# Outer products of batch 0 moved to GpSimd, two late stores moved to its queue, and a new hand-written order, in a fused sketch attention and swish layer

## The chip, the cores and the metric

The kernel runs on 1 core of one Trainium2 chip. The metric is the device time of one execution in microseconds. The profiled execution is described by its own span and its own time.

## The reference

```
q, k, v: (4, 4, 1088, 32) f32      S1, S2: (8, 32)
phi(x)[i, j] = (S1 x)[i] * (S2 x)[j]          # 64 features for each row of 32
kv  = sum_s phi(k)[s] (x) v[s]                # 64 x 32 for each batch and head
z   = sum_s phi(k)[s]
attn = phi(q) . kv / (phi(q) . z + 1e-6)
x   = attn, heads side by side                # (4352, 128)
h   = x @ w_in                                # w_in (128, 2048)
out = (h * sigmoid(beta * h)) @ w_out         # w_out (2048, 128), beta (2048)
```

## The kernel before

The work has two halves that run interleaved on one core: the attention of four batches, and the layer with w_in and w_out over nine chunks of tokens (eight of 512, a last one of 256), each chunk as soon as the attention has given its tokens.

All five engines are scheduled by hand. The string `ORDER` near the end of the kernel (line 919 on) lists short tokens; each token issues the instructions of one step, and every engine executes its own instructions in the order in which the tokens stand. A token late in the string can still run early, when its engine has nothing before it, and an engine waits at the first instruction whose inputs or buffers aren't ready.

The layer's tokens, each counted up by itself (W3.5 is the sixth of chunk 3):

- `W`: TensorE (PE) multiplies a chunk by columns of w_in (two matmuls of 128x512, or four of 128x256) into `wave`, L396. The PSUM pool `psm` behind it has two buffers, and `qps`, `nps` and others take theirs from it too, so a W waits for the silu, or the attention's read, two allocations back.
- `G`: ScalarE (ACT) takes the silu of one wave into an f16 tile `g`, L425 (L417 for the last). Six such tiles exist.
- `V`: PE multiplies `g` by w_out into the accumulator `moeout`, L470 (L459 and L448 for the last chunk).
- `O`: VectorE (DVE) turns a finished chunk into `o_sb`, L506, and `store` issues its DMAs, L380: one for each of four groups of 32 partitions, in packets of 128 B. A chunk that crosses batches has eight. The last chunk, tokens `O8`, is copied instead (`o_u`, L494) and stored by two DMAs, one on ACT's queue and one on SP's (L495).

The attention's tokens, with the batch in the first digit:

- `lk`, `lq`, `lv` load k, q and v on SP's queue (L109, L125). A tiny POOL memset ahead of each load (L108, L120, L122) holds it back until POOL has come that far; `lo`, `li` do so for the weights (L140, L136).
- `tk`, `tq`: DVE turns k or q (L521, L527). `kp`: PE's `kps`; `kt`: DVE turns it into `kab` (L569); `oKbn`: the outer product phi(k), a quarter each (L581, two or three rows of 128x256); `kv`: PE's `kvz` (L593). `gm`, `gc`, `wz`, `wc`: a Gram matrix (L607), its copy (L619), a product with it (L625) and the copy of that into `qw` (L634).
- `kd`, `no`, `ni`: DVE turns `kvz` (L638), SP writes it to DRAM (L643) and reads it back four times as `nd` (L652).
- `qp`: PE's `qps` from `qT` and `qw` (L660); `qa`: DVE turns it, two halves (L672); `dt`, `ds`, `sa`: the denominator and the scaling by it (L680, L690 and L693, L698); `oqbn`: the outer product phi(q), in parts of 128x512 or 128x768 (L705; batch 0 has two parts, the others four); `tbn`: DVE turns each part into `qt` (L715); `nm`: PE's `nps` from `qt` and `nd` (L732); `x`: two casts into `xT`, the layer's input (L747; L745 and L756 in batch 3).
- `wi`, `wo` scale parts of the weights; `cl` is eight POOL memsets (L208, L210, L212) that clear the padding of `kTs`, `pac` and `qw`; `sq` copies S1 and S2 into `qw` (L271).

A letter at the end of a token is the engine: v is DVE, c is ACT, g is GpSimd (POOL). The first 512 tokens of batch 0 take a short cut that isn't touched.

Of the kernel before, what the change touches and what calls it, by code (L numbers as in the profile page):

```python
# [20 lines left out]
def kernel(  # L21
# [12 lines left out]
    nc = tc.nc  # L34
# [52 lines left out]
    def sb(shape, dtype, name):  # L87
        return const.tile(shape, dtype, tag=name, name=name)
# [97 lines left out]
    mk = sb([P, H, R], F32, "mk")  # L186
# [168 lines left out]
    LASTC = len(tok_chk) - 1  # L355
# [17 lines left out]
    def store(o_sb, t0, u0, u1, queues):  # L373
        c = t0 + 32 * u0
        while c < t0 + 32 * u1:
            b, r = divmod(c, S)
            n = min(t0 + 32 * u1 - c, S - r) // 32
            u = (c - t0) // 32
            for g4 in range(4):
                queues[g4 % len(queues)].dma_start(  # L380
                    out=bass.AP(
                        tensor=out.tensor,
                        offset=out.offset + (b * S + r // 32) * DM + 32 * g4,
                        ap=[[T * DM, 32], [DM, n], [1, 32]],
                    ),
                    in_=o_sb[32 * g4 : 32 * g4 + 32, u : u + n, :],
                )
            c += n * 32
# [90 lines left out]
    def turn_out():  # L479
        ci = moe["o"]  # L480
        t0, tw = tok_chk[ci]
        nt = tw // 32
        if ci == LASTC:

            acc = moe["acc"].pop(0)
            b, r = divmod(t0, S)
            ns = P // nt
            for n, ((a, e), (cp, eng)) in enumerate(
                zip(LASTU, ((VC, nc.scalar), (VC, nc.sync)))
            ):  # L490
                u, p0 = divmod(a, P)
                p1 = p0 + e - a
                o_u = sbG1.tile([P, DM], F32, tag=f"o_u{n}", name=f"o_u{n}")
                cp(out=o_u[p0:p1], in_=acc[u][p0:p1, :P])  # L494
                eng.dma_start(  # L495
                    out=bass.AP(
                        tensor=out.tensor,
                        offset=out.offset + (b * S + T * (ns * u + p0 // nt) + r // 32) * DM,
                        ap=[[T * DM, (p1 - p0) // nt], [DM, nt], [1, DM]],
                    ),  # L500
                    in_=o_u[p0:p1],
                )
            moe["o"] += 1
            return
        o_sb = sbA.tile([P, TCH // 32, 32], F32, tag="o_sb", name="o_sb")
        nc.vector.transpose(  # L506
            out=o_sb[:, :nt, :].rearrange("p t d -> p (t d)"), in_=moe["acc"].pop(0)[:, :tw]
        )
        store(o_sb, t0, 0, nt, [nc.sync])
        moe["o"] += 1  # L510


# [335 lines left out]
    def x_A(i):  # L848
# [4 lines left out]
    V, C, G = nc.vector, nc.scalar, nc.gpsimd  # L853
# [11 lines left out]
        "s0": spread_sq,  # L865
        "xp": lambda: put_last(VC),
        "W": w1, "G": silu, "V": w2, "O": turn_out,
    }
    for e, eng, cp in (("v", V, VC), ("c", C, CC), ("g", G, GC)):
# [35 lines left out]
    for b in range(B):  # L905
# [14 lines left out]
                DO[f"kv{b}{j0}{j1}"] = lambda b=b, j0=j0, j1=j1: kv(b, j0, j1)  # L920

    ORDER = """
        cl h lqB tk00 h h h h h h h S0 Sbv Sc h h tk01 h rb rv bb by3c by2c mk tqA j2 j1 y2v y1c by0v ok04v
        j0 y0c by1c gm0 Spg Ssg s0 q00 q10 ok08g ok02v q01 ok00v ok01v kv002 gt ok03v gc0v zm li1 lm lk
        ok05g q11 tqB zc kv024 sq0 wi0v sq3 lk1 ok07g ok06g kv046 kv068 kv089 wi1v sq1 wi3g lo0 wi5g dA0 iA0
        kqc nq kd0 nc dA1 nA0 wi4g xA0 wi2g no0 lq1 lo1 iA1 nA1 sq2 W G wz0 wc0v xA1 wi7g tk1 W G wi6g ni0
        qp0 wo0g qa00 qa01 W W G kp1 lv1 W dt0v ds0 wo1g wo3g kt1 sa0g oq01v wo2c tq1 oq00g oK12g V V t01
        gm1 G G W gc1c wz1 lk2 lq2 V wc1c t00 qp1 V G qa10 qa11 wo4c oK10v oK11v wo5c dt1v oK13g W G V V
        wo7g W G nm0 x00c x01c ds1 sa1v kv109 kd1 no1 W oq13g ni1 oq11g lv2 W wo6c V V lk3 G W tk2 O t13 G
        kp2 kt2 G W G V W G V oq10g t10 W G gm2 W G oq12v oK21g V t11 t12 oK20g tq2 oK23v W G lq3 V nm1 gc2c  # L930
        wz2 V V x10c wc2v qp2 x11c W qa20 V oK22g V W G W G G tk3 O qa21 kv209 kd2 W lv3 no2 V W kp3 G dt2v
        ds2 G ni2 W kt3 V sa2g oq23v G W G V oq22v W G V W gm3 W V G G W V oq20g G W oK32v t22 tq3 V t20 V O
        W oK30g gc3c wz3 G G W V G W G V V W oq21g t21 t23 nm2 oK31g V V G x20c W V x21v wc3v qp3 qa30 G W G
        V V oK33g qa31 dt3g O W G W G kv309 W G W ds3 V V W sa3g V oq31g kd3 no3 G G ni3 t31 W G oq33g t33 V
        W V oq30g W G G V W G V W G V t30 W oq32v t32 nm30 O x30v W G G W V V W V G W G G V W V V G W V W V
        G O G W G nm31 W W G V V G W V V G x31v W W G G V V xp W V W G V W V V G G W G W V V W G G V W G V W
        G V W G V W O V V G V O V O
    """
    for name in ORDER.split():
        DO[name]()  # L940
# [29 lines left out]
```

## Time and profile before

| | |
|---|---|
| runs | 102.74 us median of 3 (102.02 to 103.11) |
| profiled execution | 102.41 us, span 100.6 us |
| busy, share of the span | PE 93%, ACT 76%, DVE 60%, POOL 39% |
| granted TensorE clock | 1.00 throughout |
| first W of the layer | starts at 15.5 us |
| last matmul ends | 96.7 us |
| last packet of a store | 99.1 us |
| HBM | 9.32 MB read, 2.36 MB written |

Times in the profile are microseconds from the start of the span. PE is shown busy from a matmul's start to its modelled end, so that a matmul that follows closely hides small waits; the start-to-start distance of instructions tells more than the busy share. For a DMA, the queue's entry (SPq, ACTq) is the issue; its packets move later.

### The profile page before, as it was taken

To read this page: it belongs to the slowest core of one execution; us is meant where nothing else is said; L and a number is where in the kernel's file an instruction comes from. 1 tells how busy PE (TensorE), PEld (TensorE's weight loads), DVE (VectorE), ACT (ScalarE), POOL (GpSimd) and SP (SyncE) were. 2 spreads that over 40 slices of the span, in tenths; PEclk is the share of its full clock that TensorE was granted. 3 is DMA by queue.
4 is the path that set the end of the run, shared out by engine and by line. 5 is a ranking of instruction groups with operands and counts; after the bars stand their busy time and mean duration, and the time that the engine had idled before them with its cause. 6 is when DMAs were issued, how large, how long until landed. Compare 5 with 4: busy or idle time off the path is not lost.

```text
span 100.6 us, 3192 instructions
## 1 busy us (share of the span) xinstructions
PE 93.1 (93%) x1303; PEld 44.7 (44%) x1303; DVE 60.6 (60%) x122; ACT 76.6 (76%) x100; POOL 39.4 (39%) x76
## 2 busy tenths in 40 slices
PE   6997997895999999999999999999999999999950
PEld 2336744452573444364443434644344444445740
DVE  3479599999999895599999038458230260020220
ACT  0507835788489995599999765999979979999930
POOL 6247769689309991005996003591000000000000
PEclk9999999999999999999999999999999999999999
DMA  2999995893930249985822330511015051014053
GB/s 57 312 214 289 267 349 116 296 266 92 301 148 16 58 132 227 194 228 94 217 42 47 50 55 7 89 30 50 9 18 85 0 84 20 7 22 70 13 87 69
DMA packets 24870, 11.89 MB, mean 118 GB/s; under 512 B 18436, under 2 KB 23316, under 8 KB 24856
## 3 DMA queue, kind: packets, MB, share of 16 engines
q1 hardware_dynamic: 24656, 11.61, 47.3%
q8 instruction: 10, 0.16, 0.7%
q10 hardware_dynamic: 200, 0.08, 0.4%
q14 instruction: 4, 0.03, 0.1%
HBM read 9.32 MB, written 2.36 MB: 116 GB/s over the span
## 4 chain that ended last, share of the span: by engine, by line
PE 52%; DVE 23%; DMA 10%; SPq 5%; issue 3%; ACT 2%; POOL 1%; DVEq 0%
PE wave L396 18%; PE moeout L470 17%; PE h L222 5%; DMA k<-in_k_dram 5%; PE nps L732 4%; SPq L125 4%; DVE qT L527 3%; DMA v<-in_v_dram 3%; DVE qab L672 3%; DVE qt L715 3%; DMA ndd<-kvd 2%; DVE qo L705 2%; SPq L652 2%; PE kvz L593 1%; DVE rc L690 1%
## 5 line engine op out<-in xcount | busy, mean ns | idle before, releaser
L425 ACT ACTIVATE g<-wave 128x1024 f16<-128x1024 f32 x67 | 63.9, 1030 | 10.4 <-PE wave L396 10.1
L396 PE MATMUL wave<-xT,winp 128*128 128x512 f16 (+1 forms) x152 | 39.6, 356 | 0.7 <-DVE xT L849 0.2
L470 PE MATMUL moeout<-g,woutp 128*128 128x512 f16 (+1 forms) x136 | 35.3, 366 | 0.1
L396 PEld LDWEIGHTS <-winp 128*128 128x128 f16 x152 | 13.7, 97 | 18.2 <-issue 8.5
L470 PEld LDWEIGHTS <-woutp 128*128 128x128 f16 x136 | 12.9, 97 | 14.7 <-issue 1.3
L506 DVE STREAM_TRANSPOSE o_sb<-moeout 128x512 f32<-128x512 f32 x8 | 5.6, 706 | 18.2 <-PE moeout L470 18.1
L581 POOL TENSOR_TENSOR kp<-kab 128x512 f32<-128x512 f32 (+2 forms) x12 | 13.2, 1107 | 2.2 <-DVE kab L547 2.2
L705 POOL TENSOR_TENSOR qo<-qab 128x512 f32<-128x512 f32 (+1 forms) x9 | 12.0, 1351 | 4.3 <-DVE qab L698 4.1
L715 DVE STREAM_TRANSPOSE qt<-qo 128x512 f32<-128x512 f32 (+1 forms) x14 | 10.5, 762 | 2.7 <-POOL qo L705 2.6
L732 PE MATMUL nps<-qt,nd 32*32 32x288 f32 (+1 forms) x256 | 6.8, 384 | 0.0
L672 DVE STREAM_TRANSPOSE qab<-qps 128x576 f32<-128x576 f32 (+1 forms) x8 | 5.2, 683 | 2.6 <-PE qps L660 2.6
L705 DVE TENSOR_TENSOR qo<-qab 128x512 f32<-128x512 f32 (+1 forms) x5 | 6.0, 1209 | 0.1
L698 POOL TENSOR_TENSOR qab<-qab,rc 128x288 f32<-128x288 f32 (+1 forms) x3 | 1.8, 609 | 10.1 <-DVE rc L693 10.1
L222 PE MATMUL h<-const-bfloat16-1.0 128*128 128x512 bf16 x11 | 5.0, 625 | 0.8 <-PEq L954 0.8
L527 DVE STREAM_TRANSPOSE qT<-q 128x1088 f32<-128x1088 f32 (+2 forms) x5 | 5.3, 1060 | 0.0
L593 PEld LDWEIGHTS kvz<-kp,v 128*32 128x32 f32 x288 | 4.2, 110 | 2.0 <-issue 0.8
L593 PE MATMUL kvz<-kp,v 128*32 128x64 f32 x288 | 5.1, 221 | 0.0
L310 POOL TENSOR_TENSOR winp<-beta_bc,w_in_sb 128x256 f16<-128x256 f32 x6 | 4.3, 736 | 1.5 <-DMA w_in_sb<-in_moe_w_in_dram 1.5
L732 PEld LDWEIGHTS nps<-qt,nd 32*32 32x32 f32 x256 | 3.4, 103 | 3.2 <-issue 1.3
L660 PE MATMUL qps<-qT,qw 32*32 32x288 f32 (+1 forms) x128 | 3.0, 386 | 1.6 <-ACT woutp L335 1.2
L521 DVE STREAM_TRANSPOSE kTs<-k 128x1088 f32<-128x1088 f32 x3 | 3.9, 1294 | 0.8 <-DMA k<-in_k_dram 0.8
L306 ACT COPY beta_bc<-bb 128x512 f32<-128x512 f32 x3 | 1.7, 588 | 3.4 <-PE bb L301 3.4
(105 smaller groups left out, 75.6 us busy)
## 6 DMA issues: line engine op xcount, KB each, us to landing
v<-in_v_dram SPq DMA_DIRECT2D x12, 144.0 KB, 4.6
k<-in_k_dram SPq DMA_DIRECT2D x3, 544.0 KB, 4.9
q<-in_q_dram SPq DMA_DIRECT2D x3, 544.0 KB, 3.7
out_dram<-o_sb SPq DMA_DIRECT2D x20, 64.0 KB, 2.6
w_in_sb<-in_moe_w_in_dram SPq DMA_DIRECT2D x2, 512.0 KB
w_out_sb<-in_moe_w_out_dram SPq DMA_DIRECT2D x2, 512.0 KB, 4.4
nd<-ndd SPq DMA_DIRECT2D x16, 32.0 KB, 1.8
v<-in_v_dram SPq DMA_DIRECT2D x4, 112.0 KB
```

Source lines behind the costliest of these rows:

```text
L222: nc.tensor.matmul(out=t, lhsT=idle_w, rhs=idle_x, start=True, stop=True)
L396: nc.tensor.matmul(out=wv[:, jj // per, c : c + w], lhsT=winp[:, (j0 + jj) * P : (j0 + jj + 1) * P], rhs=xT[:, t0 + o : t0 + o + w], start ...
L425: nc.scalar.activation(out=g[:, :, :gw], in_=wv[:, :, :gw], func=ACTF.Silu)
L470: nc.tensor.matmul(out=moe["acc"][-1][:, o : o + w], lhsT=woutp[:, j0 + jj, :], rhs=g[jj], start=head and jj == 0, stop=tail and jj == jn - 1,
L506: nc.vector.transpose(out=o_sb[:, :nt, :].rearrange("p t d -> p (t d)"), in_=moe["acc"].pop(0)[:, :tw])
L527: nc.vector.transpose(out=qT2[b % 2][:, t0:t1].rearrange("p t s -> p (t s)"), in_=q_t[b][:, t0:t1].rearrange("p t d -> p (t d)"),)
L581: eng.tensor_tensor(out=cut(KP[b][:, j0:j1], [[F, n], [R, R], [1, R]]), in0=a, in1=cut(KAB[b][:, 1, j0:j1], [[R, n], [0, R], [1, R]]), op=MUL,
L593: nc.tensor.matmul(out=KVZ[b][32 * h : 32 * h + 32, :F], lhsT=v_t[b][:, h, j, :], rhs=KP[b][:, j, h, :], start=(j == 0), stop=(j == NJK - ...
L672: nc.vector.transpose(out=cut(QAB[b], [[32, 2], [32 * H, nq], [1, 32]], 64 * pr), in_=PS["qps"][pr][:, :, : 32 * nq],)
L705: eng.tensor_tensor(out=cut(QO[b][:, j0:j1], [[F, n], [R, R], [1, R]]), in0=cut(a0, [[32, n], [1, R], [0, R]]), in1=cut(a0, [[32, n], [0, ...
L715: nc.vector.transpose(out=QT[b][:, j0:j1].rearrange("p j h c s -> p (j h c s)"), in_=QO[b][:, j0:j1].rearrange("p j h f -> p (j h f)"),)
L732: nc.tensor.matmul(out=t[g // 2][32 * h : 32 * h + 32, g % 2, : 32 * nq], lhsT=ND[b][rows, h, 32 * fc : 32 * fc + 32], rhs=QT[b][rows, :nq ...
```

## The change

Three edits, in one diff:

- The stores of the last chunk but one (`ci == LASTC - 1`, chunk 7) alternate between SP's queue and POOL's, two each. All other stores stay on SP's.
- In the order, both outer products of q of batch 0, `oq00` and `oq01`, stand on POOL, one behind the other; `oq01` was on DVE, ahead of `tq1`, the turning of batch 1's q.
- The rest of the order is new. No step is added or left out; some change their engine and most change their place. `cl` goes from the very start to just before `qp0`; `sq2` goes to the start; `wc0` and `wo1` go from DVE and POOL to ACT, `wo2` and `wo6` from ACT to POOL and DVE, `wo7` from POOL to ACT; the outer products of batch 3's q go to DVE altogether, while those of batch 2 and several of k change sides; `x21` goes from DVE to ACT; `lq2` is separated from `lk2`; chunk 0's stores come ahead of the loads of batch 2's v on SP's queue; `xp` stands just before W8.0.

```diff
@@ -506,7 +506,7 @@
-        store(o_sb, t0, 0, nt, [nc.sync])
+        store(o_sb, t0, 0, nt, [nc.sync, nc.gpsimd] if ci == LASTC - 1 else [nc.sync])
@@ -920,21 +920,21 @@
     ORDER = """
-cl h lqB tk00 h h h h h h h S0 Sbv Sc h h tk01 h rb rv bb by3c by2c mk tqA j2 j1 y2v y1c by0v ok04v
+h lqB tk00 h h h h h h h S0 Sbv Sc h h tk01 h rb rv bb sq2 by3c by2c mk tqA j2 j1 y2v y1c by0v ok04v
         j0 y0c by1c gm0 Spg Ssg s0 q00 q10 ok08g ok02v q01 ok00v ok01v kv002 gt ok03v gc0v zm li1 lm lk
-ok05g q11 tqB zc kv024 sq0 wi0v sq3 lk1 ok07g ok06g kv046 kv068 kv089 wi1v sq1 wi3g lo0 wi5g dA0 iA0
-kqc nq kd0 nc dA1 nA0 wi4g xA0 wi2g no0 lq1 lo1 iA1 nA1 sq2 W G wz0 wc0v xA1 wi7g tk1 W G wi6g ni0
-qp0 wo0g qa00 qa01 W W G kp1 lv1 W dt0v ds0 wo1g wo3g kt1 sa0g oq01v wo2c tq1 oq00g oK12g V V t01
-gm1 G G W gc1c wz1 lk2 lq2 V wc1c t00 qp1 V G qa10 qa11 wo4c oK10v oK11v wo5c dt1v oK13g W G V V
-wo7g W G nm0 x00c x01c ds1 sa1v kv109 kd1 no1 W oq13g ni1 oq11g lv2 W wo6c V V lk3 G W tk2 O t13 G
-kp2 kt2 G W G V W G V oq10g t10 W G gm2 W G oq12v oK21g V t11 t12 oK20g tq2 oK23v W G lq3 V nm1 gc2c
-wz2 V V x10c wc2v qp2 x11c W qa20 V oK22g V W G W G G tk3 O qa21 kv209 kd2 W lv3 no2 V W kp3 G dt2v
-ds2 G ni2 W kt3 V sa2g oq23v G W G V oq22v W G V W gm3 W V G G W V oq20g G W oK32v t22 tq3 V t20 V O
-W oK30g gc3c wz3 G G W V G W G V V W oq21g t21 t23 nm2 oK31g V V G x20c W V x21v wc3v qp3 qa30 G W G
-V V oK33g qa31 dt3g O W G W G kv309 W G W ds3 V V W sa3g V oq31g kd3 no3 G G ni3 t31 W G oq33g t33 V
-W V oq30g W G G V W G V W G V t30 W oq32v t32 nm30 O x30v W G G W V V W V G W G G V W V V G W V W V
-G O G W G nm31 W W G V V G W V V G x31v W W G G V V xp W V W G V W V V G G W G W V V W G G V W G V W
-G V W G V W O V V G V O V O
+ok05g wi1v q11 tqB zc kv024 sq0 wi0v sq3 lk1 ok07g ok06g kv046 kv068 kv089 sq1 wi3g lo0 wi5g dA0
+wi4g iA0 kqc nq kd0 nc wi2g dA1 nA0 xA0 no0 lq1 iA1 nA1 wi6g xA1 lo1 wi7g W G W wz0 ni0 wc0c cl qp0
+tk1 wo0g qa00 wo3g G qa01 dt0v lv1 W W kp1 wo1c G wo2g W G G V V ds0 kt1 sa0g oq00g oq01g gm1 lk2
+gc1c W G oK13g wz1 wo5c V wo4c tq1 wc1v qp1 t00 W G V t01 V oK11g V qa10 W G qa11 nm0 x00c x01c
+oK10v oK12v kv109 W dt1v lq2 ds1 sa1g wo6v oq12g W wo7c V V kd1 no1 G G ni1 tk2 O W lv2 oq11g G kp2
+W G V lk3 t11 W G kt2 V oq13g oq10g t13 W gm2 W oK20g V G W V G G gc2c t12 t10 tq2 nm1 wz2 x10c V V
+wc2v x11c W oK21g qp2 V G V qa20 W O W qa21 dt2v G oK23g oK22g kv209 kd2 no2 ni2 G W V ds2 W G G V
+sa2v oq23g tk3 oq22v W V V t22 W G V oq20v G W kp3 kt3 oK31g oq21g W G G V W V G W G lq3 lv3 V O W
+t20 G gm3 W G V W t23 V V W t21 G nm2 G oK33g gc3c wz3 W wc3v x20c x21c oK32v G V V W G V tq3 qp3
+qa30 qa31 W oK30g G V V O dt3g ds3 W G W kv309 G W W kd3 V V no3 G G W V sa3v oq33v W V G oq32v ni3
+W V V oq31v G G W V W G G V W oq30v t30 t33 t32 t31 nm30 W G G O W G V V W V W V G G x30v W V W G G
+V W G V W G V O W nm31 x31v G W G W V G V W V W G V G W V V W G W V V G W V G G W V W V V G O G W G
+V xp W G V W G V W G V W O V G V V V O
```

## The prediction

> **What bounds the kernel now.** I read the page's first part, then the idle time of each engine by stretches, then the timeline of the stretch where TensorE (PE) still stands idle, and last the tail. One silu (ACT, L425, the token G) handles what one W (L396) made; one V (L470) uses it. The page:
>
> ```profile
> PE 93.1 (93%) x1303; PEld 44.7 (44%) x1303; DVE 60.6 (60%) x122; ACT 76.6 (76%) x100; POOL 39.4 (39%) x76
> ```
>
> PE is the fullest engine. The table by stretches (length, then busy time and count of PE, PEld, DVE, ACT, POOL; granted clock, DMA share, GB/s):
>
> ```profile
> 44.00:56.20 12.20, 12.12 (x90) 4.91 (x89) 11.26 (x17) 11.77 (x14) 7.97 (x6) 1.00 0.48 114
> 73.00:95.30 22.30, 22.30 (x141) 10.60 (x140) 4.47 (x6) 20.63 (x23) 0.00 (x0) 1.00 0.22 35
> ```
>
> The clock is 1.00 throughout. From 44 on ACT is nearly as full as PE (11.77 of 12.20): a W and a V take 0.43 us each on PE, 0.86 together, a silu 0.93 to 0.95 (8 in 7.60). So there the silus set the pace, and PE catches up where products of the attention hold it. An earlier start of the stretch moves both engines alike, and what is gained before it should reach the end. The one large hole of PE lies before it, in the timeline of PE:
>
> ```profile
> 22.50 0.61 PE L470 MATMUL moeout<-g,woutp 128*128 128x256 f16 x4
> 24.32 0.78 PE L660 MATMUL qps<-qT,qw 32*32 32x288 f32 x32 [1.21 <-ACT woutp L335]
> ```
>
> V0.2 ends near 23.0 and qps of batch 1 (qp1) starts at 24.32. The profile names an ACT copy that ended then, but qps also reads qT of batch 1; the timelines of DVE and POOL, and the chain that ended last, show that this was late:
>
> ```profile
> 20.21 0.85 DVE L569 STREAM_TRANSPOSE kab<-kps 128x288 f32<-128x288 f32 x2
> 20.98 1.97 DVE L705 TENSOR_TENSOR qo<-qab 128x512 f32<-128x512 f32 x1
> 22.87 1.30 DVE L527 STREAM_TRANSPOSE qT<-q 128x1088 f32<-128x1088 f32 x1
> 24.10 1.52 DVE L715 STREAM_TRANSPOSE qt<-qo 128x512 f32<-128x512 f32 x2
> ```
> ```profile
> 20.90 1.51 POOL L705 TENSOR_TENSOR qo<-qab 128x768 f32<-128x768 f32 x1
> 22.36 1.52 POOL L581 TENSOR_TENSOR kp<-kab 128x512 f32<-128x512 f32 x1
> ```
> ```profile
> 21.05 1.90 DVE qo L705
> 22.95 1.22 DVE qT L527
> 24.17 1.45 DVE qt L715 x2
> ```
>
> The outer product oq01 runs on DVE ahead of the turning of q (tq1) and takes 1.97 us beside POOL's oq00; the same 128x512 product took DVE 0.65 us at 68.82, when POOL was idle. The turning ends at 24.17, qps starts 0.15 later.
>
> **The change, part by part.**
>
> *oq01 to POOL, tq1 right after kt1.* DVE loses 1.97 ahead of tq1. tq1 now runs 21.05 to 22.3 (1.25 us, rows of L527); q of batch 1 is there (its packets landed by 19.0). wz1 must end first: W0.5 and wz1 by about 22.4, wc1 by 22.6, V0.2 by 22.85, so qp1 starts near 22.85 in place of 24.32: 1.47 earlier. On POOL oq01 comes behind oq00 (20.90 to 22.41) and ends at 23.45 (1.04 to 1.07, the undisturbed 128x512 rows). Behind it on POOL come oK13 (1.51, to 25.0) and oK11 (1.05, to 26.05), while DVE has oK10 and oK12, to 26.9. kv1 needs all four; before they were ready at 28.1 and kv1 started at 28.41. PE now goes qp1 (0.70) 23.55, W0.6 24.0, V0.3 24.43, V0.4, held to 24.65 by the ACT copies wo5, wo4 (0.65 each behind G0.5), V0.5 and W0.7 by 25.95, nm0 (1.11) from 25.95 to 27.06, kv1 from there. Its inputs: t00 22.6 to 23.5, t01 to 24.25, the two qab to 25.65; v of batch 1 landed by 24.8, nd by 22.4. Gain at nm0: 27.30 - 25.95 = 1.35.
>
> *The clears of POOL (cl) moved from 2.63 to about 17.0.* Eight memsets, 0.49 us in the trace (2.63 to 3.12). At the start POOL waited 1.88 us for st anyway: worth nothing. Now they stand behind wi6, wi7 (two at 0.70, 15.62 to 17.02) and end near 17.5; qps of batch 0 and the turning of k (tk1) wait for them. qps starts at 17.5 in place of 17.21, but its readers (qab) wait on DVE for tk1, which ends at 18.35 as before: 0 to 0.15 lost. The cover is those 0.4 us of tk1. The copy wc0 goes from DVE (0.13) to ACT (0.17, between two silus): W0.2 moves from 18.12 to 18.3, but W0.3 waits for the first qab (18.8) either way. sq2 (0.19) now precedes sk and spm on POOL; spm ends by 6.3, and its user starts at 9.28: nothing.
>
> *The new order after that.* Same instructions, moved. I went by hand through the places where an input may come late, with the rows' durations.
> - nm1: POOL does sa1, oq12, oq11, oq13, oq10 in a row from 28.35 (0.65, 1.07, memsets 0.4, 1.07, 1.51, 1.07: 34.2); the last turn ends at 35.3; PE arrives at 35.35. Start 35.4 for 37.04: 1.6 gained, with no margin.
> - SP's queue: k and q of batch 2 no longer go together, q follows oK11 at 26.1, ahead of no1 at 28.9: free. Chunk 0's stores (four at 0.55) now stand ahead of v and k of batches 2 and 3: v then lands near 39.4 (issue 35 to 38; before 38.5), kv2 starts at 41.3: covered by 1.9. tk3, which waited 0.84 us for k before, stands later on DVE.
> - kv2 ends at 42.5 for 43.89 (1.4). Then silus set the pace: G2.3 starts at 43.0 for 44.53 (1.5).
> - nm2 waits for oq21, on POOL behind oK31, which waits for kt3 on DVE: 48.85, 49.9, 51.0, its turn 53.1; PE arrives at 53.7. Covered by 0.6, which DVE products slowed by POOL (1.2 for 0.9, twice) would use up.
> - Batch 3: all four outer products on DVE, POOL idle by then: 0.95 + 3 x 0.65 from 62.85, turns to 68.6; PE reaches nm30 at 69.0. If POOL's absence didn't help (1.27 each, the mean of L705 DVE 128x512) nm30 would wait 1.5 us.
> This gives 1.4 to 2.0 at these places. It grants every handover at the trace's best, so I count 1.4 from the first stage and 0.3 from the order.
>
> *Two stores of chunk 7 on POOL.* The tail:
>
> ```profile
> 95.39 1.95 SPq L380 DMA_DIRECT2D out_dram<-o_sb  x4
> 97.43 0.61 SPq L495 DMA_DIRECT2D out_dram<-o_u  x1
> ```
> ```profile
> 96.69 0.52 DVE L494 COPY o_u<-moeout 128x128 f32<-128x128 f32 x2 [1.33 <-PE moeout L448]
> ```
>
> The last store is issued 0.22 after its copy ended (97.21), as SP is busy until 97.34. With two stores fewer it goes out at 97.27: 0.16 gained, perhaps 0.3, since its packets then stand behind 1024 others of 128 B and not 2048. The price of a store issued by POOL is in no row. Lower end: SP's median, 0.46 us. Upper end: 2.0, the longest instruction of either vector engine on a 128x512 tile (1.97). I take 1.07, POOL's own time for 512 elements a partition, as a store has 512 packets. SP's last packet left 1.24 us after its last issue ended (98.58 after 97.34), so POOL's would leave at 95.4 + 2 x 1.07 + 1.24 = 98.8, just ahead of the last packet of all (99.14): nothing lost, and the 0.15 stays. At 2.0 it is 100.6: 1.5 lost.
>
> A rule of the Trainium skill speaks against this part: "DMA: Bandwidth & Descriptors", section "Issuing engines are not separate DMA queues", says that stores of any engine end on the same 16 DMA engines, and that spreading them only saves issue time; its Specifications give about 1 us to the first byte for POOL's path and 0.6 for SP's. By that the part is worth at most the 0.16 and may cost an estimated 0.4 us at the start of POOL's packets, which the 0.3 us of slack above nearly hides.
>
> **Sum.** 1.4 + 0.3 + 0.15 = 1.85 off the profiled execution's 102.41 (span 100.6 and 1.8 around it, unchanged): 100.56. It lies 0.33 under the median of the runs, 102.74, so 100.9 in such a median. With the bounds: from 2.3 gained to, with POOL's stores at 2.0 each, 0.2 gained.
>
> **Rivals.**
> 1. *The gain is taken back* by new waits at nm1, nm2 and nm30 (no margin, 0.6, 0.4): two of them late by 0.5 to 0.8 leave 1.85 - 1.2 = 0.65: 102.1. For: POOL's and DVE's products ran at 1.27 on the mean and not at 1.07 and 0.65. Against: in this order fewer of them overlap. 0.21.
> 2. *POOL's stores set the end* (slower). Their place is the last 5 us, with nothing behind them to hide in. From 1.25 us each they end after today's last packet; from 2.1 us they have eaten the gain; at 3.0 the end is 96.64 + 6.0 = 102.64 for 99.14, 3.5 later, less 1.7: 104.5. For: no row bounds them. Against: POOL's elementwise work on as many elements takes half of that. 0.12.
> 3. *The stall doesn't go*: qp1 really waited for the ACT copies, which the profile names. They then end at 24.6, qp1 starts no earlier, and only about 0.45 remains: 102.3. Against: qps reads nothing that they write. 0.05.
>
> **How the numbers follow.** The forecast, 100.9 (own range 100.0 to 101.6), has 0.62. A measurement tells about 1% from no change, 1.03 us. Faster by more: 0.62 and a little of rival 1, 0.64. Within 1%: most of rivals 1 and 3, 0.23. Slower: rival 2 and a little beside, 0.13. The range, 99.9 to 102.9, takes in rivals 1 and 3 and POOL's stores up to 2.2 us each; the slow end of rival 2 is left out.
>
> **What would show it.** Right: PE's hole before the second qps under 0.3 us, that qps near 22.9, the first nps near 26, the second near 35.4, nm2 near 53.8; the last o_u store issued within 0.1 of its copy, POOL's two stores under 1.2 us each. Wrong: a hole of over 0.5 us ahead of a later nps or kvz, ACT with as many gaps after 44 as now, or a last packet that is POOL's.

## The result, and the profile after

The changed kernel takes 101.58 us in the median (100.70 to 104.44, 22 runs), the kernel before 102.19 us (101.16 to 103.91, 22 runs) beside it. The ratio is 0.994, with a 95% interval of 0.9919 to 0.9962: faster by 0.6%, where the forecast was 1.8%. The profiled execution took 101.3 us (span 99.5), 1.1 us under that of the kernel before, and the forecast for it was 1.85. So even the two profiles differ by more than the medians do. In some executions the full TensorE clock comes several us later than in others; the ratios leave these out, and below places are counted from the first W of the layer, which takes most of that out.

The page of the changed kernel, busy time by engine, and the table by stretches (columns as before):

```profile
PE 92.0 (92%) x1303; PEld 44.7 (45%) x1303; DVE 58.2 (58%) x123; ACT 77.2 (78%) x101; POOL 37.6 (38%) x76
```
```profile
44.00:56.20 12.20, 12.18 (x149) 5.29 (x147) 7.56 (x12) 11.10 (x14) 6.55 (x8) 1.00 0.40 107
73.00:95.30 22.30, 22.30 (x159) 11.24 (x157) 3.79 (x5) 21.00 (x24) 0.98 (x2) 1.00 0.23 37
```

DVE lost 2.4 us and the picture is otherwise the same: PE is the fullest engine, and in the last stretch ACT has a little more to do (21.00 for 20.63). The place of the large hole, in the timelines of PE, DVE and POOL:

```profile
22.63 0.61 PE L470 MATMUL moeout<-g,woutp 128*128 128x256 f16 x4
23.17 0.77 PE L660 MATMUL qps<-qT,qw 32*32 32x288 f32 x32
...
26.13 1.18 PE L732 MATMUL nps<-qt,nd 32*32 32x160 f32 x64
```
```profile
20.40 0.82 DVE L569 STREAM_TRANSPOSE kab<-kps 128x288 f32<-128x288 f32 x2
21.14 1.27 DVE L527 STREAM_TRANSPOSE qT<-q 128x1088 f32<-128x1088 f32 x1
```
```profile
21.10 2.54 POOL L705 TENSOR_TENSOR qo<-qab 128x768 f32<-128x768 f32 x2
```

The hole of 1.21 us before qps of batch 1 is gone: qps follows V at 23.17, the turning of q directly follows kab on DVE, and both outer products run on POOL in 2.54. Against the profile of before all this is as forecast, and it is the wrong comparison, as the experiments show.

The tail, as the timelines of SP's and POOL's queues, and two rows of the DMA views (a queue's packets, MB and share; an issue's KB each and median us to landing):

```profile
94.03 0.85 SPq L380 DMA_DIRECT2D out_dram<-o_sb  x2
95.87 0.62 SPq L495 DMA_DIRECT2D out_dram<-o_u  x1
```
```profile
94.32 1.47 POOL L380 DMA_DIRECT2D out_dram<-o_sb  x2 [32.88 <-DVE o_sb L506]
```
```profile
q0 software_dynamic: 64, 0.13, 0.8%
```
```profile
out_dram<-o_sb SPq DMA_DIRECT2D x18, 64.0 KB, 2.0
...
out_dram<-o_sb POOLq DMA_DIRECT2D x2, 64.0 KB, 2.7
```

The last store goes out 0.03 us after its copy's end (95.84), as forecast. But the span ends 4.01 us after the last matmul, where it was 3.71. (In the profile of before the last matmul ends at 96.88 us, 96.27 and 0.61 in its timeline; the 96.7 of the table ahead is too early.)

### The profile page after: what moved, and what is told of

It reads as the page before. It is cut to its first block, busy times and chain, and to the rows that moved or that the text cites. A ratio compares the mean times of both kernels' runs of the same rounds, so it can differ in the third digit from the quotient of the medians.

```text
span 99.5 us, 3187 instructions
## 1 busy us (share of the span) xinstructions
PE 92.0 (92%) x1303; PEld 44.7 (45%) x1303; DVE 58.2 (58%) x123; ACT 77.2 (78%) x101; POOL 37.6 (38%) x76
## 4 chain that ended last, share of the span: by engine, by line
PE 75%; DMA 10%; POOL 4%; ACT 3%; DVE 1%; issue 1%; SPq 1%
PE wave L396 31%; PE moeout L470 27%; PE nps L732 7%; DMA w_in_sb<-in_moe_w_in_dram 5%; DMA q<-in_q_dram 5%; PE kvz L593 3%; POOL winp L310 3%; PE qps L660 2%; PE kps L558 2%; ACT g L425 2%; PE moeout L459 1%; ACT xT L747 1%; PE gram L607 1%; SPq L109 1%; DVE qT L527 1%
## 5 line engine op out<-in xcount | busy, mean ns | idle before, releaser
L425 ACT ACTIVATE g<-wave 128x1024 f16<-128x1024 f32 x67 | 63.8, 1032 | 9.0 <-PE wave L396 8.9
L380 POOL DMA_DIRECT2D out_dram<-o_sb x2 | 1.5, 736 | 32.9 <-DVE o_sb L506 32.9
L705 POOL TENSOR_TENSOR qo<-qab 128x512 f32<-128x512 f32 (+1 forms) x8 | 9.8, 1233 | 5.5 <-DVE qab L698 5.4
L715 DVE STREAM_TRANSPOSE qt<-qo 128x512 f32<-128x512 f32 (+1 forms) x14 | 10.0, 760 | 1.3 <-POOL k L108 1.1
L222 PE MATMUL h<-const-bfloat16-1.0 128*128 128x512 bf16 x11 | 4.2, 537 | 0.8 <-PEq L954 0.8
L705 DVE TENSOR_TENSOR qo<-qab 128x512 f32<-128x512 f32 (+1 forms) x6 | 4.5, 785 | 0.0
L747 ACT CAST xT<-nps 128x576 f16<-128x576 f32 (+1 forms) x6 | 3.4, 568 | 1.3 <-PE nps L732 1.2
```

The lines of the kernel that those rows point to most:

```text
L425: nc.scalar.activation(out=g[:, :, :gw], in_=wv[:, :, :gw], func=ACTF.Silu)
L705: eng.tensor_tensor(out=cut(QO[b][:, j0:j1], [[F, n], [R, R], [1, R]]), in0=cut(a0, [[32, n], [1, R], [0, R]]), in1=cut(a0, [[32, n], [0, ...
L715: nc.vector.transpose(out=QT[b][:, j0:j1].rearrange("p j h c s -> p (j h c s)"), in_=QO[b][:, j0:j1].rearrange("p j h f -> p (j h f)"),)
```

## The experiments

**The first set: the parts of the change.** The changed kernel again; the clears back at the very start; all stores on SP's queue; and the kernel before with only `oq01` on POOL.

> The changed kernel again, for a second profile. Theory A (the profiled executions of before and after differ by 1.11 us, but the TensorE clock was granted in full from 6.28 us in the one and from 3.74 us in the other, which moved the first W from 15.50 to 15.05): the ratio stays 0.994 within 0.003, and the time of the first W goes with the moment of the full clock, 15.0 to 15.6. Rival (the clears taken from the start make the start shorter): first W at 15.05 within 0.1 whatever the clock. Both: a wait of qps of batch 0 for the POOL clears of 0.7 to 1.1 us, as long as w_in's second half lands at 13.3 to 13.9.

Ratio to the kernel before 0.9952 (0.9919 to 0.9986). Its profile: first nps at 10.56 after the first W, last matmul ending at 79.93 after it, tail (from there to the end of the span) 3.98. In the changed kernel's first profile the same two were 11.08 and 80.47, as w_in had landed late and the second W waited 0.41 us for POOL: its figures are the less typical ones.

```diff
-h lqB tk00 ... wc0c cl qp0
+cl h lqB tk00 ... wc0c qp0
```

> The changed kernel with the eight clears of POOL back at the very start. Theory A (the clears, queued on POOL behind the weights' scaling and so behind the landing of w_in, cost the 0.7 us that are missing between the first W and qps of batch 1): qps of batch 0 starts within 1.7 us of the first W in place of 2.79, qps of batch 1 at most 7.7 us after the first W in place of 8.12, the ratio to before goes from 0.994 to 0.989. Theory B (VectorE's turning of k and the second W, which waits for POOL's scaled weights, bind anyway): the qps hole goes, but qps of batch 1 stays at 8.0 to 8.2 us after the first W and the ratio at 0.994. Theory C (the start needs POOL free): the first W comes 0.3 to 0.45 later, ratio 0.997.

0.9927 (0.9889 to 0.9966), no different within the intervals. qps of batch 0 starts 1.76 after the first W and not 2.27, but qps of batch 1 comes at 7.57, for 7.60 with late clears: the turning of k on DVE hides the delay, as the prediction had it.

```diff
-        store(o_sb, t0, 0, nt, [nc.sync, nc.gpsimd] if ci == LASTC - 1 else [nc.sync])
+        store(o_sb, t0, 0, nt, [nc.sync])
```

> The changed kernel with all four stores of chunk 7 on SP's queue. Theory A (POOL's two stores cost: their 32 large packets of 300 to 560 ns hold the DMA engines until 97.4, while the o_u stores want them): from the last matmul's end to the end of the span 3.9 us, as before (3.93), in place of 4.19; no packet of 4096 B; ratio 0.992. Theory B (SP's free queue is worth the 0.16 us by which o_u's store goes out earlier): 4.35, ratio 0.9955.

0.9898 (0.9849 to 0.9948) from few runs, so it was run again below. The tail is 3.76: 0.22 to 0.25 us come back.

```diff
-... sa0g oq01v wo2c tq1 oq00g oK12g V V t01 ... wc1c t00 qp1
+... sa0g wo2c tq1 oq00g oq01g oK12g V V t00 ... wc1c t01 qp1
```

> The kernel before with one part of the change alone: oq01 on POOL behind oq00, t00 ahead of t01, all else as before. Theory A (this part carries the gain, and the clears take half of it back in the whole change): qps of batch 1 starts 7.2 to 7.6 us after the first W (8.82 before, 8.12 after), the last matmul ends 1.0 to 1.4 earlier, ratio 0.988. Theory B (the part needs the new order behind it, since kv of batch 1 then waits for POOL's outer products of k, 1.05 later each): qps of batch 1 comes early, but a hole of 0.5 to 1.0 us opens ahead of kvz of batch 1, ratio 0.994 to 1.0.

1.0031 (0.9993 to 1.0069): no gain at all from the edit that the prediction gave 1.4 us. Against the profile of before, qps of batch 1 does come 1.29 earlier (7.53 after the first W, for 8.82) and the first nps 1.30. Then PE waits for DVE's outer products of k and for a turn:

```profile
28.03 0.99 PE L593 MATMUL kvz<-kp,v 128*32 128x64 f32 x56 [0.39 <-DVE kp L581]
...
36.88 1.52 PE L732 MATMUL nps<-qt,nd 32*32 32x288 f32 x55 [0.45 <-DVE qt L715]
```

and 0.31 is left at the last matmul. I read this as a gain handed back; the third set shows that in most executions there was none to hand back.

**The second set: POOL's stores, and POOL ahead of qps.** The two stores alone in the kernel before; SP's stores again; these with the clears first; and these with `wi2` and the clears ahead of `wi5` on POOL.

> The kernel before with one part of the change alone: two stores of chunk 7 on POOL's queue. Theory A: from the last matmul's end to the end of the span 3.95 to 4.0 us in place of 3.72, all else the same, ratio 1.002. Theory B (the prediction's: o_u's store goes out 0.16 earlier and the rest follows): 3.55, ratio 0.998.

1.0041 (0.9999 to 1.0083), tail 4.02 for 3.71. Over all sets, the five profiles with POOL's stores have a tail of 3.98 to 4.03, the fifteen without them 3.71 to 3.76. That is 0.27 us lost on the mean, in the old order and in the new. Up to its last stores this kernel is the kernel before, and its profile has the hole too, 1.18 us ahead of qps of batch 1:

```profile
20.83 1.95 DVE L705 TENSOR_TENSOR qo<-qab 128x512 f32<-128x512 f32 x1
```
```profile
20.72 1.51 POOL L705 TENSOR_TENSOR qo<-qab 128x768 f32<-128x768 f32 x1
```

> The changed kernel with all four stores of chunk 7 on SP's queue, again, for its time (the first had four undisturbed runs, and its profile a late clock). Theory A (POOL's stores cost 0.25): tail 3.7, ratio 0.9915 to 0.993 where the changed kernel has 0.994 to 0.995. Theory B (they are worth nothing either way): 0.9945.

0.991 (0.9874 to 0.9946), last matmul at 79.88.

> The changed kernel with the clears at the very start and all stores on SP's queue; wi2 stays behind wi5 and wi4. Theory A (half of POOL's chain is gone, 0.45 of 3.94): qps of batch 0 at 1.7 to 1.9 us after the first W unless w_in lands late, qps of batch 1 at 7.5 to 7.6, ratio 0.989 to 0.991. Theory B (the clears at the start delay what follows): as with all stores on SP's queue alone or 0.002 slower.

0.9915 (0.9884 to 0.9946), last matmul at 79.97.

```diff
-sq1 wi3g lo0 wi5g dA0 ... nc wi2g dA1 ... wc0c cl qp0
+sq1 wi3g lo0 wi2g cl wi5g dA0 ... nc dA1 ... wc0c qp0
```

> The changed kernel with all stores on SP's queue, and on POOL wi2 and the eight clears moved ahead of wi5, into the 1.8 to 2.5 us in which POOL waits for the second half of w_in. Theory A (qps of batch 0 starts 3.94 us after w_in has landed, in both profiles of the changed kernel, since wi5, wi4, wi2, wi6, wi7 and the clears stand between): qps of batch 0 no longer moves with w_in and starts 1.6 to 1.8 us after the first W (2.27 and 2.79 before), the second W directly behind the first, qps of batch 1 at 7.2 to 7.5 us after the first W, span tail 3.72, ratio to the kernel before 0.985 to 0.988. Theory B (VectorE's turning of k, 1.3 us, covers the wait but for 0.2): qps of batch 1 at 7.5 to 7.6, ratio as with all stores on SP's queue alone, 0.990.

0.9929 (0.9896 to 0.9962), last matmul at 80.28: no gain from POOL's order there.

These left a gap. The versions with SP's stores end 1.4 to 1.5 us before the profile of before, counted from the first W, but are faster by 0.9 to 1.0 us only (1.1 and 0.7 with `wi2` moved).

**The third set: the start, or the kernel before itself.** The changed kernel with SP's stores and the old start; the kernel before with the new start; the kernel before again; and `before_oq01` with `wo7` on ACT and not on POOL between the outer products.

```diff
-h lqB tk00 ... bb sq2 by3c ... ok05g wi1v q11 ... kv089 sq1 ... nA1 wi6g ... wc0c cl qp0
+cl h lqB tk00 ... bb by3c ... ok05g q11 ... kv089 wi1v sq1 ... nA1 sq2 wi6g ... wc0c qp0
```

> The changed kernel with all stores on SP's queue and with the start of the kernel before: the clears first, sq2 behind nA1, wi1 behind kv089; the order from the first W on is the new one. Open: with its stores on SP the changed kernel ends 1.45 to 1.50 us earlier than the kernel before when both are counted from their first W, but the ratios are 0.990 to 0.991, some 1.0 us. Theory A, the new start itself makes the first W about 0.4 us later: ratio 0.986 to 0.987 here, first W near 15.4 to 15.5. Theory B, the first W moves from run to run with the landing of the first loads and the moment at which the full clock is granted, whatever the order: ratio 0.990 to 0.992, the first W anywhere between 15 and 16.1, and the stretch from there to the last matmul 79.9 to 80.0 as in the other two versions.

0.9894 (0.9853 to 0.9935), last matmul at 80.07: the old start brings nothing that the intervals can tell.

> The kernel before with the start of the changed one alone: the clears just before qp0, sq2 behind bb, wi1 ahead of q11. Theory A (the new start costs about 0.4 us): ratio near 1.004. Theory B (it costs nothing by itself): 0.999 to 1.001, first W by landing and clock as in the other runs. For both: qps of batch 0 waits for POOL's clears some tenths of a us, which the turning of k of batch 1 on DVE covers; last matmul 81.3 to 81.6 after the first W.

1.0018 (0.9978 to 1.0058), so it isn't shown that the new start costs 0.4 us, nor that it doesn't. In its profile the granted clock was half from 18.49 to 21.90 us, so its places aren't used.

> The kernel before once more, for its second profile: how far its first W and the moment of the full clock move from run to run. Theory A: first W again within 0.2 of 15.50. Theory B: it may move by as much as the changed kernel's (15.05 to 16.1), and the stretch from the first W to the last matmul stays at 81.4.

This profile shows why. The same kernel has no hole: qps of batch 1 at 7.56 after the first W, first nps at 10.54, as early as in the changed kernel (7.60, 10.56). Its timelines of DVE and POOL:

```profile
20.14 0.78 DVE L569 STREAM_TRANSPOSE kab<-kps 128x288 f32<-128x288 f32 x2
20.84 0.65 DVE L705 TENSOR_TENSOR qo<-qab 128x512 f32<-128x512 f32 x1
21.41 1.29 DVE L527 STREAM_TRANSPOSE qT<-q 128x1088 f32<-128x1088 f32 x1
```
```profile
20.84 2.02 POOL L705 TENSOR_TENSOR qo<-qab 128x768 f32<-128x768 f32 x1
```

DVE's product takes 0.65 and POOL's 2.02, where the first profile had 1.97 and 1.51. There POOL's was recorded as starting 0.08 ahead of DVE's (20.90 and 20.98); here both start at 20.84. One of the two runs through and the other stands.

> The kernel before with oq01 on POOL and one step more of the new order: the scaling wo7 on ACT ahead of wo6 and no longer on POOL between the outer products. With oq01 alone the 1.30 us gained at the first nps was handed back in two places, 0.39 before kvz of batch 1 (DVE's outer products of k) and 0.45 before its nps (DVE's turns). Theory 1, the products of batch 1 themselves are the limit (their sides and order, as the new order changes them): kvz starts 0.1 to 0.3 earlier, nps of batch 1 within 0.2 of 21.3 after the first W, ratio 0.999 to 1.003. Theory 2, POOL's work beside DVE's is the limit: with wo7's 1.07 gone, nps of batch 1 comes at 20.4 to 20.8 and the end 0.7 to 1.0 earlier, ratio 0.991 to 0.994.

0.9994 (0.9956 to 1.0031). The nps of batch 1 comes at 20.53 after the first W, as theory 2 said, but the last matmul ends at 81.06, as with `oq01` alone (81.07): what is gained there doesn't reach the end.

**The fourth set: who starts first.** The kernel before with one memset more, on POOL ahead of `oq00` or on DVE ahead of `oq01`, and two more profiles of it.

```diff
-... sa0g oq01v wo2c tq1 oq00g
+... sa0g oq01v wo2c tq1 dg oq00g        # dg: a memset of 128x128 on POOL
```

> The kernel before with one memset of 128x128 more on POOL, between its scaling sa0 and its outer product oq00, so that DVE's outer product oq01 always starts ahead of POOL's. In the second profile of the kernel before both started at 20.84 and DVE's took 0.65 and POOL's 2.02; in the first POOL's started at 20.90 and DVE's at 20.98, and DVE's took 1.97 and POOL's 1.51. Theory of the toss: whichever is first runs through and the other stands until it is done. Then here DVE's takes 0.65, POOL's about 2.0 from its start on, no hole before qps of batch 1, which comes 7.5 to 7.6 after the first W, last matmul at 80.8; the time is 0.1 to 0.6 us under that of the kernel before, depending on how often that one loses: ratio 0.994 to 0.999. Rival (the 1.97 has another cause, the second profile was luck): DVE's takes anything between 0.65 and 1.97, ratio 1.000 within 0.002.

1.0021 (0.9976 to 1.0066). DVE's product took 0.69, POOL's 1.99, and qps came at 7.84 without a hole. It is not faster than the kernel before. That doesn't tell how often the kernel before has the hole, as this one loses time elsewhere: its last matmul, at 81.61, is late because PE stood 0.77 us at 54.23 behind a chunk's turning on DVE.

```diff
-... sa0g oq01v wo2c tq1 oq00g
+... sa0g dv oq01v wo2c tq1 oq00g        # dv: a memset of 128x128 on DVE
```

> The kernel before with one memset of 128x128 more on DVE, between the turning of kab and the outer product oq01, so that POOL's oq00 always starts ahead. Theory of the toss: DVE's oq01 takes 1.3 more than 0.65, less its delay, POOL's 1.51, a hole of 1.2 before qps of batch 1, which comes 8.8 after the first W, last matmul at 81.4; the time is 0.6 us above that of the version with DVE first, ratio to the kernel before 1.000 to 1.005. Rival (another cause): the same as the version with DVE first within 0.002.

0.9995 (0.9954 to 1.0037). It didn't do what it was for: POOL's product was recorded 0.14 us ahead, but DVE's took 0.63 and POOL's 2.13. Whether DVE's memset, 0.06 after POOL's start, made it lose stays open.

> The kernel before, third profile, to see how often the stall comes. Theory of the toss: qps of batch 1 at 8.8 after the first W with DVE's outer product at about 1.97, or at 7.55 with 0.65, nothing between. Rival: other durations and places.

> The kernel before, fourth profile, with the same expectation as the third: qps of batch 1 at 8.8 after the first W with DVE's outer product at about 1.97, or at 7.55 with 0.65, nothing between.

In both DVE's product took 0.65 and POOL's 2.03, and qps of batch 1 came at 7.71 and 7.70. So the profile that the prediction rests on is the one of four with the stall; with `before_poolst`, which is the same up to its last stores, it is two of five (and `before_newstart`, with the clock at half just before, has it as well). So few profiles don't tell the share closely.

**The fifth set: the stall put there, and the edit undone.** A turning instead of the memset on DVE; and the changed kernel with `oq01` back on DVE ahead of `tq1`.

```diff
-... sa0g oq01v wo2c tq1 oq00g
+... sa0g dt oq01v wo2c tq1 oq00g        # dt: a turning of 128x128 on DVE (its input is cleared by POOL at the start)
```

> The kernel before with one turning (transpose) of 128x128 more on DVE between kt1 and the outer product oq01, where the version with a memset missed: there POOL's outer product was recorded as starting 0.14 us ahead, and DVE's still ran through (0.63, POOL's 2.13). DVE's turnings have run beside POOL's products at no loss to either, so this one should leave the start to POOL. Theory of the toss: POOL's oq00 takes 1.51, DVE's oq01 stands until it is over (1.6 to 1.9 in all), qps of batch 1 comes 8.8 to 8.9 after the first W, the last matmul 81.4 to 81.7, ratio 1.002 to 1.007. Rival (the duration of DVE's product is not decided by who is first): oq01 at 0.65 again, qps of batch 1 at 7.7 to 7.9, ratio 0.999 to 1.001.

1.0068 (1.0025 to 1.0112): with the stall put there for good, the kernel before is slower than it usually is. Not all of the 0.7 us is the stall's: the turning itself takes 0.27 on DVE, and the last matmul, at 81.84, is 0.46 behind that of the stalled profile of before. DVE's and POOL's timelines, and PE's:

```profile
20.91 0.27 DVE L870 STREAM_TRANSPOSE idle_b<-idle_a 128x128 f32<-128x128 f32 x1
21.10 1.78 DVE L705 TENSOR_TENSOR qo<-qab 128x512 f32<-128x512 f32 x1
```
```profile
20.83 1.51 POOL L705 TENSOR_TENSOR qo<-qab 128x768 f32<-128x768 f32 x1
```
```profile
24.25 0.78 PE L660 MATMUL qps<-qT,qw 32*32 32x288 f32 x32 [1.21 <-ACT woutp L335]
```

The hole is back to the hundredth (1.21), and qps is at 8.82 after the first W.

```diff
-... kt1 sa0g oq00g oq01g gm1 ...
+... kt1 sa0g oq01v oq00g gm1 ...
```

> The changed kernel with oq01 alone back on DVE, ahead of the turning of batch 1's q, and all the rest as changed: the edit that the change is named after is undone. In three of four profiles of the kernel before, DVE's product won its start and took 0.65 us, and the first nps then came as early (10.54 to 10.68 after the first W) as in the changed kernel (10.56). Theory C (that edit is worth little in most executions, the later order makes the gain): ratio 0.993 to 0.997, last matmul 79.9 to 80.6 after the first W, as in the changed kernel; if the profile shows the toss lost, qps of batch 1 at 8.8 and half a us of it left at the end. Theory D (my forecast: oq01 on POOL is worth 1.4 us): ratio 1.003 to 1.008.

0.9935 (0.9898 to 0.9972), the same as the changed kernel's 0.994; last matmul at 80.11. In its profile DVE's product won (0.69, POOL's 2.02). Theory C held: within the interval, some 0.4 us either way, the edit that the change is named after is worth nothing, and the rest of the order makes the gain.

## Why the prediction was wrong, point by point

**The term that failed: "I count 1.4 from the first stage".** The mechanism is real. DVE's `oq01` beside POOL's `oq00` can hold back `tq1`, qps and nps, and putting it on POOL takes this away: against the profile of before, qps of batch 1 came 1.22 earlier in `after_again` (forecast 1.47), the first nps 1.24 (forecast 1.35). What failed is the base. The sum took a stall from one execution and then added 0.33 to stand against the median, as if every run had it. Three of four profiles of the kernel before have none, and against these the term is 10.54 to 10.69 less 10.56 at the first nps: 0.13 at most. Most of the signs that the prediction named for being right did appear (no hole, the second qps at 23.17, the first nps at 26.13), and the forecast failed all the same: they tell where the changed kernel stands, and not how often the kernel before has the stall. That the direction came out right is in part luck, as the gain comes from a term counted at 0.3.

The ends show whether DVE or POOL had gone first. Wherever DVE's product lost and the clock was full, in the profile of before, in `before_poolst` and in `before_pool_first2`, it ended 0.54 to 0.55 us after POOL's had ended, close to its own 0.65, and POOL's took 1.51. Wherever it won, POOL's ended 1.36 to 1.38 after DVE's, and DVE's took 0.63 to 0.69. So nearly all of the loser's work is done behind the winner's end, and 0.08 us of recorded start can decide 1.3 us. The Trainium skill, "SBUF — State Buffer", section "SBUF: two separate sides", states this as a rule: a VectorE operation with two SBUF inputs and a GpSimd operation that reads SBUF take a shared pair of ports by an exclusive lock, and whoever starts first has it for the whole instruction. The trace agrees with it in these rows, but for `before_pool_first`, where POOL's recorded start was 0.14 ahead and DVE's product ran through; that stays open. The rule would have told me that a 1.97 beside a 1.51 is a lost start and not a slow product. What makes DVE late by those 0.08 (the turning of kab before it took 0.85 in these three profiles and in `before_dve_first`, and 0.78 in the other profiles in which DVE's product won) stays open.

The stall costs less at the end than where it stands, too. The start of chosen silus (L425), read from the trace in us after each kernel's first W:

| silu | before, stalled | before again | changed, again | `after_oq01v` |
|---|---|---|---|---|
| G0.7 | 11.96 | 10.71 | 10.73 | 10.94 |
| G1.7 | 21.23 | 19.98 | 20.03 | 20.33 |
| G2.3 | 29.03 | 28.31 | 27.83 | 28.01 |
| G2.7 | 32.92 | 32.20 | 32.18 | 32.36 |
| G3.3 | 36.61 | 35.88 | 35.80 | 35.98 |
| G4.3 | 47.83 | 47.25 | 46.39 | 46.57 |
| last | 80.20 | 79.62 | 78.75 | 78.93 |

Of 1.25 at G0.7, 0.72 is left at G2.7 and 0.58 at the end (0.40 and 0.37 at the last matmul against the third and fourth profiles of before). The step "an earlier start of the stretch moves both engines alike, and what is gained before it should reach the end" held for less than half: without the stall, PE of the kernel before waits 0.43 us before the nps of batch 1 for DVE's turn in two profiles, and 0.54 before kvz in the other.

**The order, forecast 0.3, measured 0.87** (79.62 less 78.75; against the third and fourth profiles of before, 1.05 and 1.08 at the last matmul). The table tells where. By G2.3 0.48 is gained, and gone again by G2.7. Then, between G3.3 and G4.3, 0.8 is gained that stays. In that stretch ACT of the kernel before, in its second profile, stands idle in five gaps, 2.54 us together; in the changed one there are four, 1.49 together, though ACT does one cast more there (0.64, `x21`, which was on DVE). The timelines of PE there, before (first) and changed (second):

```profile
55.46 1.60 PE L732 MATMUL nps<-qt,nd 32*32 32x288 f32 x64
56.99 1.04 PE L470 MATMUL moeout<-g,woutp 128*128 128x512 f16 x4
57.87 0.59 PE L396 MATMUL wave<-xT,winp 128*128 128x512 f16 x2
```
```profile
54.07 1.60 PE L732 MATMUL nps<-qt,nd 32*32 32x288 f32 x64
55.60 0.25 PE L625 MATMUL wz<-gs,lw 128*32 128x8 f32 x8
55.78 0.61 PE L396 MATMUL wave<-xT,winp 128*128 128x512 f16 x2
56.22 1.03 PE L470 MATMUL moeout<-g,woutp 128*128 128x512 f16 x4
```

And ACT's silus behind them:

```profile
57.06 0.64 ACT L747 CAST xT<-nps 128x576 f16<-128x576 f32 x1 [0.41 <-PE nps L732]
58.56 1.02 ACT L425 ACTIVATE g<-wave 128x1024 f16<-128x1024 f32 x1 [0.85 <-PE wave L396]
```
```profile
55.67 1.31 ACT L747 CAST xT<-nps 128x576 f16<-128x576 f32 x2 [0.34 <-PE nps L732]
56.88 1.95 ACT L425 ACTIVATE g<-wave 128x1024 f16<-128x1024 f32 x2
```

In the old order two V follow the nps and ACT waits 0.85 us for the W behind them. In the new one a W comes first, ACT does both casts meanwhile, and its next two silus then follow without a gap. I looked at that place only for whether nm2's inputs come in time (they do: 38.74 after the first W, and no wait), not for what ACT does behind it. No run changed this place alone, so it is read from the timelines. That the gain needs neither the new start nor `oq01` on POOL is shown, each undone by itself, by `after_oldstart_sp` and `after_oq01v`.

**The tail, forecast 0.15 gained, measured 0.27 lost.** The two parts that I named came out: the last store is issued 0.19 sooner behind its copy (0.03 for 0.22, forecast 0.16), and a POOL store takes 0.74 us (1.47 for two), inside the bounds of 0.46 to 2.0 and under the 1.07 taken. "Nothing lost" failed at the packets. In the changed kernel's first profile POOL's two stores move as 32 packets of 4096 B, each taking 0.16 to 0.83 us, between 96.05 and 97.60, the first 1.73 us after the first issue. The 512-B packets of the two `o_u` stores move at the same time, from 96.97 on. The first of these stores takes 0.82 us from first to last packet in place of 0.45, and the last packet of all leaves 2.15 us after the copies' end in place of 1.93. That POOL's stores cost this is shown by the versions with and without them; that they do so by holding DMA engines is read from the times. The rule of the Trainium skill that the prediction cited ("DMA: Bandwidth & Descriptors", section "Issuing engines are not separate DMA queues") had the right sign: stores of every queue share the engines. Its later start, an estimated 0.4 us, agrees when it is counted from the end of the first issue for the chunk: the first packet comes 0.92 us behind POOL's and 0.53 behind SP's. Counted from the start of the issue it is 1.73 against 0.84, as POOL's first issue takes longer too (0.82 for 0.32).

**The sum, made again.** From the unstalled executions: nothing for the first stage, 0.87 gained by the order and 0.27 lost at the end, 0.6 in all. That is the measured 0.6%, but the close fit is in part luck: with the third or fourth profile of before it is 0.8, and the interval of the measurement is 0.4 to 0.8 us. With SP's stores it is 0.87, for 0.9 to 1.1 us in the four measurements without the move of `wi2`. The two edits alone don't speak against it: `oq01` in the kernel before moves its last matmul from 80.80 (80.98 and 81.01 in the third and fourth profiles) to 81.08 and its time by +0.3%, and the stores alone cost 0.4%, both with intervals that take in no change.

**The rivals.** Rival 1, the gain taken back by new waits at nm1, nm2 and nm30, isn't what happened: no nps of the changed kernel waits. Rival 2 has the right place and sign, but 0.27 us for two stores and not 3.5. Rival 3 was right only in that the hole needn't cost the time, for another reason than the ACT copies. The clears cost nothing, as said, save in one profile where w_in came late.

The best version is the changed kernel with all stores on SP's queue, 0.9894 to 0.9915 in four measurements of three forms (as it is, with the clears first, with the old start); the intervals don't tell these apart.

## What to carry to other kernels

Before a stall from one profile is put into a sum, ask whether another execution would have it: two instructions of VectorE and GpSimd that start within 0.1 us of each other, one of them drawn out by about the length of the other, are a race that the next execution may win, and a second profile of the unchanged kernel is the cheapest experiment there is. In a chain in which one engine feeds another, look at what the fed engine does behind each block of other work: by the timelines, putting a W ahead of two V there was worth more than the hole that the eye went to. Keep late stores off a queue whose packets are large and slow, even when the issue itself looks cheap.

## What the runs showed of the hardware

- An elementwise product on DVE and one on POOL stood for each other for whole instructions, 0.65 or 1.97 us for the same work on DVE and 1.51 or 2.03 on POOL, while DVE's turnings beside POOL's products (0.78 and 1.27) showed no such loss.
- Two stores of 64 KB issued by POOL became 32 packets of 4096 B and landed 2.7 us after their issue, where those of SP's queue, in packets of 128 B, took 2.0.
- The first W came between 15.05 and 16.34 us in profiles of these two kernels, with the full clock granted at any time between 3.55 and 6.28 us and the first load of q landing between 6.41 and 7.03 us: enough by itself to hide or feign 1%. The moment of the clock alone doesn't set it, as the latest first W went with the earliest clock (16.34 and 3.55).
